# Batch 0 of a fused RWKV and low-rank-mixing kernel: V spread from two fp32r parts, and the last chunk's share of U·x added in 128-column pieces

## The chip, the cores and the metric

The kernel runs on one core of a Trainium2 chip. The metric is the device time of one execution in microseconds; lower is better. All engines named below are those of this core: PE (TensorE, with PEld for its weight loads), DVE (VectorE), ACT (ScalarE), POOL (GpSimd) and SP (SyncE), the last of which issues most DMAs.

## What is computed

There are 4 batches, 768 positions, 8 heads of 48 channels (so 384 channels), a hidden width of 1536 and a rank of 32. Cut to what matters, the reference is:

```
for t in range(S):                                   # attention, per batch and head
    y[t]  = r[t] @ (state + (u * k[t]) outer v[t])
    state = w * state + k[t] outer v[t]
x  = y as [batch, 768, 384]
h  = x^T @ U @ V                                     # U 768x32, V 32x768
u_ = x + h^T
out = u_ + relu(u_ @ w_ch1) @ w_ch2                  # 384 -> 1536 -> 384
```

U, V, w_ch1 and w_ch2 arrive as 64-bit floats and are turned into 32-bit ones on the chip; the outputs are 32-bit.

## The kernel before, in words

The positions of a batch are cut into 6 chunks of 128. For each chunk the attention is computed in products of chunk size: scores from r and k (`f_scores`, L1003), a masked copy of them (`am`, L1011), the change of the state (`f_state`, L1025), the product of masked scores with v (`f_out`, L1052) and of r with the carried state (L1058). DVE adds the two halves of a chunk's output to the term of u and writes x_0 to x_5 (L1071). Batch 0 has nothing to run beside it; the attention of batches 1 to 3 runs between products of the batch before.

What follows for a batch is low-rank mixing and then the two large products. G = U^T x (32 x 384) is summed over the chunks (`g_sum`, L1171): four products of 32 output rows each stand side by side in one PSUM bank, and in batch 0 the sum lies in the bank `wake`, which also takes filler products. `c_g` copies the four pieces into one SBUF tile `gf` and makes `Gs` of it, three blocks of 32 rows: G rounded to fp32r, the rest that rounding left, and the rounded G once more. `V3` (96 x 768) holds V in the same way in three blocks: rounded, rounded, rest. One product of K = 96 of `V3` and `Gs` then gives V·G almost as exactly as 32-bit inputs would. `c_x` transposes the chunks of x into banks (`pu`, and `bank_sc` and `bank_tr` for the second half of the batch), `c_xu` (`pu<-V,Gs`) adds V·G on top, ACT rounds the sum into `uTh` and DVE puts the rest into `uTl`. Those are the inputs of the first large product (`m_1`, `p1`), which takes three products per 128 x 128 block: weights high and low with `uTh`, weights high with `uTl`. ACT applies the relu (`hh`), DVE the rest (`hl`), and `m_2` (`p2`) multiplies by the second weights. The two halves of batch 0 (384 positions each) are t = 0 and t = 1.

V is loaded as a 128 x 192 tile (`raw_v`: 4 groups of 32 rows hold 192 columns of V each) and has to be spread to 32 x 768, three times over. `v_split` does that with four 32-bit products against `sel`, a 0-1 matrix, two for each half of V3; ACT casts a half and DVE subtracts the rounded block from the third.

Every weight tile that is loaded (`raw_w`) needs a byte pass (L605 on ACT or L601 on DVE), a scaling pass (L627, ACT) and two bit passes (L608 and L611, DVE) to become a 32-bit float, and then a cast (L645, ACT) and a subtraction (L646, DVE or POOL) to become a high and a low part, `w1s` or `w2s`.

The order of all engines is written out by a planner (`Plan.schedule`): the program records every operation with its key (`at(t, f)`), an estimated length and its buffers, and the planner lists the operations engine by engine as its estimates come out. It may choose POOL, DVE or ACT for operations that are given alternatives, and it puts filler products (`wake`, `wake2`) where it expects TensorE to idle. So a changed estimate or key moves operations far from the edit. Dependencies become semaphore waits; each engine runs its list strictly in that order.

## Time and profile before

| what | value |
|---|---|
| median of 3 runs | 400.66 us (399.52 to 400.8) |
| profiled execution, its own time | 400.29 us |
| its span, first to last instruction | 398.6 us |
| mean granted TensorE clock | 0.999 |
| PE busy | 389.6 us, 98% of the span |
| PEld busy | 374.7 us, 94% |
| DVE busy | 301.5 us, 76% |
| ACT busy | 143.8 us, 36% |
| POOL busy | 99.8 us, 25% |

The span is what the trace covers; the execution's own time is 1.7 us longer than it. A busy time is the sum of the stretches in which an engine executes at least one instruction; filler products count as busy, and successive products overlap, so that a product's listed length is longer than the distance to the next one. A share of the whole span says little of a single stage: in the first 50 us of this kernel, where batch 0's attention ends and its large products begin, the engines are used differently from the 350 us behind it.

### The profile page before, as it was taken

How to read it: one execution, taken by the hardware profiler on the slowest of the kernel's cores; microseconds unless marked ns; L12 is line 12 of the kernel's file. 1: busy time of each engine (PE TensorE's matmuls, PEld its weight loads, DVE VectorE, ACT ScalarE, POOL GpSimd, SP SyncE). 2: the span in 40 equal slices, each digit the busy share in tenths (PEclk: the TensorE clock that was granted, in tenths of full speed). 3: DMA queues.
4: the chain of work that ended last, by engine and by line, in shares of the span. 5: the costliest groups of instructions: out<-in, count | busy, mean ns of one | idle time of the engine just before them, and what ended most of it. 6: DMA issues, size and time to landing. Idle time of an engine off the chain costs nothing.

```text
span 398.6 us, 11762 instructions
## 1 busy us (share of the span) xinstructions
PE 389.6 (98%) x4815; PEld 374.7 (94%) x4815; DVE 301.5 (76%) x681; ACT 143.8 (36%) x372; POOL 99.8 (25%) x152
## 2 busy tenths in 40 slices
PE   7999999999999999999999999999999999999995
PEld 6897899999999999999999999999999999999994
DVE  5798999999999768888684588999444874555453
ACT  3557968467841312110133240241132422232220
POOL 2972142244422014131140131544000301100000
PEclk9999999999999999999999999999999999999999
DMA  9989998698769685785797777800126110000003
GB/s 143 177 174 276 176 222 191 107 231 213 133 99 198 99 193 78 124 134 81 147 168 111 150 167 114 136 6 3 61 46 137 57 62 0 2 0 2 0 0 127
DMA packets 189995, 45.28 MB, mean 114 GB/s; under 512 B 174702, under 2 KB 188399, under 8 KB 189935
## 3 DMA queue, kind: packets, MB, share of 16 engines
q1 hardware_dynamic: 186382, 43.28, 57.9%
q10 hardware_dynamic: 3552, 1.18, 1.4%
q8 instruction: 40, 0.66, 0.7%
q14 instruction: 21, 0.16, 0.2%
HBM read 36.77 MB, written 7.67 MB: 111 GB/s over the span
## 4 chain that ended last, share of the span: by engine, by line
PE 93%; DVE 3%; DMA 2%; SPq 0%; issue 0%; ACT 0%; DVEq 0%
PE p L385 63%; PE c L385 9%; PE pav L900 3%; PE pav L906 3%; PE bank_tr L385 2%; PE bank_sc L385 2%; DMA ld<-in_r_dram 2%; PE pav L1052 2%; PE bank_tr L1003 1%; PE bank_tr L880 1%; PE bank_tr L866 1%; PE bank_tr L1171 1%; PE pav L1058 1%; PE ptr L817 1%; DVE uTl L1235 1%; PE psu L1025 1%
## 5 line engine op out<-in xcount | busy, mean ns | idle before, releaser
L385 PE MATMUL p<-uTh,w1s 128*128 128x384 f32 x432 | 112.0, 339 | 0.2 <-DVE w1s L646 0.2
L385 PE MATMUL p<-w2s,hh 128*128 128x384 f32 x528 | 111.8, 339 | 0.2 <-ACT hh L1445 0.2
L385 PEld LDWEIGHTS p<-w2s,hh 128*128 128x128 f32 x528 | 92.3, 188 | 1.7 <-ACT hh L1445 0.7
L1445 ACT ACTIVATE hh<-p 128x384 fp32r<-128x384 f32 x72 | 35.4, 492 | 144.0 <-PE p L385 143.9
L385 PEld LDWEIGHTS p<-uTh,w1s 128*128 128x128 f32 x432 | 76.9, 188 | 1.3 <-DVE w1s L646 0.6
L385 PE MATMUL p<-uTl,w1s 128*128 128x384 f32 x216 | 72.5, 336 | 0.0
L1446 DVE SCALAR_TENSOR_TENSOR hl<-p,hh 128x384 fp32r<-128x384 f32 x72 | 39.9, 554 | 31.5 <-ACT hh L1445 30.7
L385 PE MATMUL p<-w2s,hl 128*128 128x384 f32 x264 | 62.3, 335 | 0.0
L385 PEld LDWEIGHTS p<-w2s,hl 128*128 128x128 f32 x264 | 47.3, 188 | 0.0
L385 PEld LDWEIGHTS p<-uTl,w1s 128*128 128x128 f32 x216 | 40.5, 188 | 0.3 <-DVE uTl L1235 0.3
L900 PEld LDWEIGHTS pav<-vsw,am 64*64 64x64 f32 x288 | 17.4, 134 | 4.5 <-issue 4.3
L1372 ACT ACTIVATE hh<-v 128x384 fp32r<-128x384 f32 x18 | 9.2, 526 | 34.4 <-DVE v L1363 31.7
L900 PE MATMUL pav<-vsw,am 64*64 64x48 f32 x288 | 19.8, 221 | 0.0
L1363 DVE TENSOR_TENSOR v<-c,s 128x384 f32<-128x384 f32 x18 | 9.9, 556 | 12.9 <-PE c L385 12.7
L900 PE MATMUL pav<-ldv,am 64*64 64x48 f32 x288 | 19.3, 221 | 0.0
L767 POOL MEMSET ks<- 128x128 f32 x24 | 4.8, 208 | 57.2 <-PE bank_tr L880 57.2
L906 PE MATMUL pav<-S,rT 48*64 48x48 f32 x528 | 19.1, 218 | 0.0
L1283 POOL TENSOR_TENSOR uTl<-ut,uTh 128x384 fp32r<-128x384 f32 x5 | 5.1, 1022 | 54.1 <-ACT uTh L1282 54.1
L385 PE MATMUL c<-uTh,w1s 128*128 128x384 f32 x72 | 18.5, 337 | 0.0
L777 POOL TENSOR_TENSOR dv<-ldr,ldk 128x384 f32<-128x384 f32 x13 | 13.3, 1022 | 20.4 <-DVE wm L528 8.8
L906 PEld LDWEIGHTS pav<-S,rT 48*64 48x64 f32 x528 | 17.3, 135 | 0.0
L900 PEld LDWEIGHTS pav<-ldv,am 64*64 64x64 f32 x288 | 17.0, 134 | 0.0
(240 smaller groups left out, 782.4 us busy)
## 6 DMA issues: line engine op xcount, KB each, us to landing
raw_w<-in_moe_w_ch_dram SPq DMA_DIRECT2D x24, 384.0 KB, 4.7
out_dram<-x SPq DMA_DIRECT2D x21, 192.0 KB, 2.9
ldr<-in_r_dram SPq DMA_DIRECT2D x20, 192.0 KB, 3.9
ldk<-in_k_dram SPq DMA_DIRECT2D x20, 192.0 KB, 4.8
ldv<-in_v_dram SPq DMA_DIRECT2D x20, 192.0 KB, 4.7
bl<-in_r_dram SPq DMA_DIRECT2D x79, 48.0 KB, 2.4
bl<-in_k_dram SPq DMA_DIRECT2D x79, 48.0 KB, 2.5
ub<-ud SPq DMA_DIRECT2D x15, 192.0 KB, 2.9
```

The lines of the kernel that those rows point to most:

```text
L385: return nc.tensor.matmul(*args, **kw)
L767: op("POOL", 250, lambda: nc.gpsimd.memset(ks.t[:, :, D:], 0.0), [(ks, "pad")], [])
L777: on_either(384, lambda e, a_=a_, b_=b_: e.tensor_mul(dv.t, a_()[:, :, :D], b_()[:, :, :D]), w_, r_, only="POOL" if front(n) else None)
L817: nc.tensor.transpose(pt.t[:PD, q * C:(q + 1) * C], src().rearrange("p h d -> p (h d)")[:, q * PE_:q * PE_ + PD], ident_)
L900: return nc.tensor.matmul(to(q, j, i), lhsT=am[j].t[half, q, :], rhs=vsw[n].t[half, q, :] if j else vt()[half, 2 * q, :], start=((alone or ...
L906: return nc.tensor.matmul(to(q, row, i), lhsT=rT.t[rows, q, i * C2:(i + 1) * C2], rhs=St[n, i].t[rows, q, :], start=False, stop=((alone or ...
L1052: return nc.tensor.matmul(avp[n][j].t[i * C2:(i + 1) * C2, q * D:(q + 1) * D], lhsT=ams[n][j].t[:, q, i * C2:(i + 1) * C2], rhs=vt()[:, 2 ...
L1283: on_either(384, lambda e: e.tensor_tensor(ul.t[:, ct, :], ut.t, f32(uh.t[:, ct, :]), ALU.subtract), [(ul, ct)], [ut, (uh, ct)])
L1363: on_dve(384, lambda e: e.tensor_tensor(to.t, pt.t[:, :TB], other.t, ALU.add), [to], [pt, other])
L1372: on_act(384, lambda: nc.scalar.activation(hh.t, value(), AF.Relu), [hh], [src])
L1445: on_act(384, lambda: nc.scalar.activation(hh.t, pt.t[:, :TB], AF.Relu), [hh], [pt])
L1446: on_dve(384, lambda e: e.scalar_tensor_tensor(hl.t, pt.t[:, :TB], 0.0, f32(hh.t), ALU.max, ALU.subtract), [hl], [pt, hh])
```

## The change

There are four parts.

1. **V.** `raw_v` is split into two fp32r parts, `v_parts` (ACT casts, POOL or DVE subtracts), and each half of V3 is the sum of four fp32r products of 192 columns, two for each part, against `sel` with blocks of zeros around the identity. What arrives in the bank is already (rounded, rounded, rest), so the cast by ACT is all that is left and DVE's subtraction falls away. The second half of V3 (t = 1) is recorded later, behind the first `p1`.
2. **G.** The sum over the chunks 0 to 4 is copied to `gf` before the last chunk is done (`c_g_sum`), and one 32-bit product against `sel` writes it three times into a bank (`pG_0` in `bank_tr`). When x_5 is there, three 32-bit products of 128 columns add the last chunk (`c_g_last`), and `Gs` is cast by ACT and finished by DVE column piece by column piece. `c_xu` of batch 0 waits for its own piece and its own half of V3.
3. **The first `p1`** takes its products in another order, those with the late low parts last.
4. **Estimates and keys.** The planner's lengths for several TensorE operations are raised (103 to 116 a transposition, 500 to 550, 520 to 600, 1000 to 1060), the keys of `G` and V are moved, the refill uses the still tile, and the chunks of batches 2 and 3 are recorded 3 us later.

```diff
-    Uf = cbuf([128, NCH, 1, R], F32, "Uf")
+    Uf = cbuf([128, NCH + 2, 1, R], F32, "Uf")
-    sel = wbuf([128, 3 * 128], F32, "xh", NXS, "sel")
+    sel = big([128, 128 // R, 6, R], F32R, "sel")
...
         def v_split(fl, raw):
-            for j in range(S // DM):
+            vp = big([128, 2, NV], F32R, "v_parts")
+            on_act(NV, lambda: nc.scalar.copy(vp.t[:, 0], fl()), [(vp, 0)], [raw])
+            on_either(NV, lambda e: e.tensor_tensor(vp.t[:, 1], fl(), f32(vp.t[:, 0]), ALU.subtract), [(vp, 1)], [raw, (vp, 0)])
+
+            def half(j):
                 pt = bank("acc", f"pv_{j}")
...
-                        whole(pt.t[:3 * R, i * NV:(i + 1) * NV],
-                              lhsT=sel.t[:, c * 3 * R:(c + 1) * 3 * R], rhs=fl(),
-                              start=(i == 0), stop=(i == DM // NV - 1), skip_group_check=True)
+                        for k, b0 in enumerate((3, 0)):
+                            whole(pt.t[:3 * R, i * NV:(i + 1) * NV], lhsT=sel.t[:, c, b0:b0 + 3], rhs=vp.t[:, k],
+                                  start=(i + k == 0), stop=(i + k == DM // NV), skip_group_check=True)
...
-                on_dve(384, lambda e, sl=sl, pt=pt: e.tensor_tensor(V3.t[2 * R:, sl], pt.t[2 * R:3 * R, :DM],
-                                                                    f32(V3.t[2 * R:, sl]), ALU.subtract), [(V3, j)], [pt])
+            half(0)
+            v_rest.append(lambda: half(1))
...
+    def c_g_sum():
+        w4 = DM // 4
+        gf = wbuf([R, DM], F32, "xl", NXS, "gf_0")
+        for g in range(4):
+            on_act(96, lambda g=g: nc.scalar.copy(gf.t[:, g * w4:(g + 1) * w4], wk.t[g * R:(g + 1) * R, 128:128 + w4]),
+                   [(gf, g)], [(wk, "g")])
+        pt = bank("tr", "pG_0")
+        pg.append(pt)
+        pe(700, lambda: whole(pt.t[:3 * R, :DM], lhsT=f32(sel.t[:R, 0, 2:5]), rhs=gf.t, start=True, stop=False, skip_group_check=True),
+           [(pt, ct) for ct in range(NCT)], [gf, sel])
+
+    def c_g_last():
+        n, pt = NCH - 1, pg[0]
+        three = Uf.t[:, n:].rearrange("p c o r -> p (c o r)")
+        G = Gs[0] = wbuf([3 * R, DM], F32R, "Gs", 1, "Gs_0")
+        for ct in range(NCT):
+            cs = slice(ct * 128, (ct + 1) * 128)
+            pe(235, lambda cs=cs, ct=ct: whole(pt.t[:3 * R, cs], lhsT=three, rhs=xs[n].t[:, cs], start=False, stop=(ct == NCT - 1),
+                                               skip_group_check=True), [(pt, ct)], [Uf, xs[n]])
+            on_act(128, lambda cs=cs: nc.scalar.copy(G.t[:, cs], pt.t[:3 * R, cs]), [(G, ct)], [(pt, ct)])
+            on_dve(128, lambda e, cs=cs: e.tensor_tensor(G.t[R:2 * R, cs], pt.t[R:2 * R, cs], f32(G.t[R:2 * R, cs]), ALU.subtract),
+                   [(G, ct)], [(pt, ct)])
...
+        if (b, t, f) == (0, 0, 0):
+            for ct, k in ((0, 0), (1, 0), (0, 2), (2, 0), (1, 2), (2, 2)):
+                pe((2 - k // 2) * MM, lambda ct=ct, k=k: part(ct, (2,) if k else (0, 1)), [pt], [((ul if k else uh), ct), W1[f]])
...
-    UV, GX, UVC = -84.9, (3, 33.0), (25.0, 33.0)
+    UV, GX, UVC = -84.9, (3, 32.0), (25.0, 31.6)
...
-                at(t, lambda n=n: a_chunk(n))
+                at(t + (0, 0, 3, 3)[b], lambda n=n: a_chunk(n))
...
+            at(end - 3, c_g_sum)
+            at(end, c_g_last)
+            at(t + 1.9, lambda: v_rest[0]())
```

What the planner makes of it is shown at three places. In the rows the number at a tile's end is its buffer's; 0 to 5 before it, in x, am, kT, ld and pav, is the chunk.

The first place is ACT while PE computes chunks 4 and 5 of batch 0. kT is the copy of a chunk's transposed k, without which the scores of that chunk can't start; L605 and L627 are the first two passes over a loaded tile. Before:

```order
L840 COPY kT_4_507<-ptk_4_489 112x512
L605 ACTIVATE raw_u_395<-raw_u_395 128x192
L627 ACTIVATE raw_u_395<-raw_u_395 128x192
L605 ACTIVATE raw_v_425<-raw_v_425 128x192
L627 ACTIVATE raw_v_425<-raw_v_425 128x192
L1041 ACTIVATE SW_4_567<-S_4_554,wmf_155 112x48 x4
L840 COPY kT_5_599<-ptk_5_583 112x512
L651 COPY Uf_617<-raw_u_395 128x192
L605 ACTIVATE raw_w1_0_477<-raw_w1_0_477 128x384
L627 ACTIVATE raw_w1_0_477<-raw_w1_0_477 128x384
```

Now:

```order
L605 ACTIVATE raw_u_378<-raw_u_378 128x192
L846 COPY kT_4_496<-ptk_4_479 112x512
L627 ACTIVATE raw_u_378<-raw_u_378 128x192
L605 ACTIVATE raw_v_398<-raw_v_398 128x192
L627 ACTIVATE raw_v_398<-raw_v_398 128x192
L1047 ACTIVATE SW_4_546<-S_4_544,wmf_158 112x48 x4
L605 ACTIVATE raw_w1_0_455<-raw_w1_0_455 128x384
L627 ACTIVATE raw_w1_0_455<-raw_w1_0_455 128x384
L846 COPY kT_5_593<-ptk_5_575 112x512
L652 COPY Uf_91<-raw_u_378 128x192
L653 COPY Uf_91<-raw_u_378 128x64
```

kT_5 stood ahead of the first weight tile's two passes and now stands behind them; kT_4 likewise stands behind one pass over raw_u.

The second place is PE from the end of chunk 5's attention to the first product of V3 and Gs; wake2 is a filler. Before, without the ten rows of transpositions into pu and bank_sc that stand between the two pieces:

```order
L385 MATMUL pv_0_742<-raw_v_425,sel_103 96x192 x2
L385 MATMUL pv_1_752<-raw_v_425,sel_103 96x192 x2
L1171 MATMUL wake_101<-x_5_748,Uf_617 32x96 x4
```

```order
L385 MATMUL pu0_0_2_787<-ident_69,x_2_473 128x128
L385 MATMUL wake2_794<-V3_756 128x512
L385 MATMUL bank_tr_88<-ident_69,x_4_663 128x128
L385 MATMUL bank_sc_89<-ident_69,x_5_748 128x128
L385 MATMUL pu0_1_1_774<-ident_69,x_5_748 128x128
L385 MATMUL bank_tr_88<-ident_69,x_5_748 128x128
L385 MATMUL wake2_794<-V3_756 128x512
L385 MATMUL pu0_0_0_766<-V3_756,Gs_0_791 128x384
```

Now, with the semaphores that each waits for:

```order
L385 MATMUL bank_tr_88<-gf_0_683,sel_104 96x384 [waits Activation_49]
L385 MATMUL bank_sc_89<-ident_69,x_3_561 128x128
L385 MATMUL bank_sc_89<-ident_69,x_4_657 128x128
L385 MATMUL bank_tr_88<-x_5_738,Uf_91 96x128 [waits DVE_49]
L385 MATMUL pv_0_753<-v_parts_728,sel_104 96x192 [waits Activation_49]
L385 MATMUL pv_0_753<-v_parts_728,sel_104 96x192 [waits Pool_49]
L385 MATMUL pv_0_753<-v_parts_728,sel_104 96x192 x2
L385 MATMUL bank_tr_88<-x_5_738,Uf_91 96x128 [waits Activation_49]
L385 MATMUL bank_tr_88<-x_5_738,Uf_91 96x128 [waits DVE_49]
```

The nine transpositions of t = 0, one filler of 128 columns and `pu<-V3,Gs` follow. The second and third column pieces of the last chunk's sum wait for ACT and DVE to be done with the first, and everything behind them on PE with them. The transpositions of t = 1 and its three products with V3 and Gs, which stood ahead of the first p1, now stand behind the second p1, and the second half of pv between the two.

The third place is ACT from its last passes over early weight tiles to the first uTh. Before:

```order
L627 ACTIVATE raw_w2_1_615<-raw_w2_1_615 128x384
L665 CAST V3_756<-pv_0_742 96x384
L665 CAST V3_756<-pv_1_752 96x384
L1191 COPY gf_0_771<-wake_101 32x96 x4
L1193 CAST Gs_0_791<-gf_0_771 32x384
L1196 CAST Gs_0_791<-gf_0_771 32x384
L645 CAST w1s_0_804<-raw_w1_0_477 128x384
L645 CAST w1s_1_806<-raw_w1_1_494 128x384
L1234 CAST uTh_0_0_813<-pu0_0_0_766 128x384
```

Now:

```order
L1206 COPY gf_0_683<-wake_102 32x96 x4
L605 ACTIVATE raw_w2_1_570<-raw_w2_1_570 128x384
L657 CAST v_parts_728<-raw_v_398 128x192
L627 ACTIVATE raw_w2_1_570<-raw_w2_1_570 128x384
L605 ACTIVATE raw_w1_2_605<-raw_w1_2_605 128x384
L627 ACTIVATE raw_w1_2_605<-raw_w1_2_605 128x384
L1222 CAST Gs_0_759<-bank_tr_88 96x128
L671 CAST V3_763<-pv_0_753 96x384
L1222 CAST Gs_0_759<-bank_tr_88 96x128 x2
L646 CAST w1s_0_780<-raw_w1_0_455 128x384
L646 CAST w1s_1_788<-raw_w1_1_471 128x384
L1263 CAST uTh_0_0_794<-pu0_0_0_767 128x384
```

The copies of gf moved ahead of the last chunk, and two tiles' passes and the cast of V's high part now stand between them and the first piece of Gs. On DVE (no rows) the two subtractions of V3 and one byte pass are gone from the same stretch, three short pieces of Gs stand where one of 384 columns stood, and the three uTl of t = 1 moved behind the third weight tile's passes.

## Rows read from the trace of the kernel before

**Rows 1.** Waits of PE: engine, tile, line, releaser: us in total, times, longest.

```profile
PE pu L385 <- DVE Gs L1194: 0.5, 1, 0.5
```

**Rows 2.** Busy time by stretch: stretch, length, busy (instructions) by engine, clock, DMA share, GB/s.

```profile
33.00:48.00 15.00, 13.62 (x132) 11.75 (x129) 13.70 (x31) 12.07 (x31) 1.62 (x5) 1.00 1.01 217
48.00:100.00 52.00, 52.00 (x698) 50.45 (x697) 51.08 (x119) 34.93 (x100) 18.87 (x25) 1.00 0.91 193
...
390.00:399.00 9.00, 3.63 (x21) 3.19 (x19) 2.14 (x4) 0.53 (x1) 0.00 (x0) 0.93 0.28 98
```

**Rows 3.** The chain of waits, 33 to 48 us: start, us, what.

```profile
35.64 0.62 DVE x L1071 x2
...
37.23 1.03 DVE V L666 x2
...
40.31 0.43 PE pu L385
...
40.76 0.49 ACT uTh L1234
...
46.96 0.48 DVE w1s L646
```

**Rows 4.** Timeline of PE, 15 to 33 us: start, us, instruction, tile shapes, count.

```profile
15.50 0.49 PE L385 MATMUL wake<-still 128*128 128x128 f32 x2
15.90 0.43 PE L817 MATMUL ptr<-ident,ld 128*112 128x128 f32 x2
...
30.48 0.37 PE L1003 MATMUL bank_tr<-rT,kT 48*128 48x128 f32 x1
```

**Rows 5.** Timeline of ACT, 29 to 38 us; in brackets idle time before, and its releaser.

```profile
29.11 0.57 ACT L840 COPY kT<-ptk 112x512 f32<-112x512 f32 x1
...
29.85 0.57 ACT L605 ACTIVATE raw_w<-raw_w 128x384 int32<-128x384 uint8 x1
30.32 0.55 ACT L627 ACTIVATE raw_w<-raw_w 128x384 f32<-128x384 f32 x1
30.79 0.57 ACT L605 ACTIVATE raw_w<-raw_w 128x384 int32<-128x384 uint8 x1
...
34.45 0.56 ACT L605 ACTIVATE raw_w<-raw_w 128x384 int32<-128x384 uint8 x1 [1.40 <-DMA raw_w<-in_moe_w_ch_dram]
...
37.45 0.95 ACT L1191 COPY gf<-wake 32x96 f32<-32x96 f32 x4
```

**Rows 6.** Timeline of PE, 33 to 48 us.

```profile
33.84 0.20 PE L1052 MATMUL pav<-ldv,am 128*64 128x48 f32 x1 [0.65 <-issue]
33.98 0.33 PE L385 MATMUL bank_tr<-ident,x 128*128 128x128 f32 x1
34.24 0.67 PE L1052 MATMUL pav<-ldv,am 128*64 128x48 f32 x16
...
35.45 1.59 PE L385 MATMUL pv<-raw_v,sel 128*96 128x192 f32 x8
36.97 0.37 PE L1171 MATMUL wake<-x,Uf 128*32 128x96 f32 x8
...
37.99 0.93 PE L385 MATMUL pu<-ident,x 128*128 128x128 f32 x7
38.67 0.48 PE L385 MATMUL wake<-V 96*128 96x512 f32 x1
...
41.44 0.51 PE L385 MATMUL p<-uTh,w1s 128*128 128x384 f32 x2
...
42.17 0.51 PE L385 MATMUL p<-uTh,w1s 128*128 128x384 f32 x2
42.52 0.33 PE L385 MATMUL p<-uTl,w1s 128*128 128x384 f32 x1
...
46.91 0.34 PE L385 MATMUL p<-uTh,w1s 128*128 128x384 f32 x1
47.48 0.44 PE L385 MATMUL p<-uTh,w1s 128*128 128x384 f32 x1 [0.24 <-DVE w1s L646]
```

More of the change, by code (lines that the diff above doesn't have):

```diff
@@ L634, in rwkv_moe @@
     BANKS = [None] * 26
+    v_rest, pg = [], []
     def weight_units():
@@ L820, in a_tr @@
         for q in range(0, NP, m):
-            pe(103 * m, lambda q=q: turn(q, q + m), [pt], sb)
+            pe(116 * m, lambda q=q: turn(q, q + m), [pt], sb)
         def by_pair():
@@ L1004, in product @@
                                     start=True, stop=True)
-        pe(1000, lambda: in_turn(*([lambda q=q, j=j: product(q, j) for q in range(NP)] for j in range(2))), abs_[n], [rT, kT],
+        pe(1060, lambda: in_turn(*([lambda q=q, j=j: product(q, j) for q in range(NP)] for j in range(2))), abs_[n], [rT, kT],
            tiled=True)
@@ L1172, in g_sum @@
                                  rhs=xs[n].t[:, g * w4:(g + 1) * w4],
-                                 start=(c0 == 0 and n % NCH == 0), stop=(n % NCH == NCH - 1), skip_group_check=True)
+                                 start=(c0 == 0 and n % NCH == 0), stop=(n % NCH == NCH - (1 if n >= NCH else 2)), skip_group_check=True)
     def c_gx(*ns):
@@ L1181, in c_g @@
         w4 = DM // 4
-        if b:
-            bank_ = bank("tr", f"pG_{b}")
-            pt, c0 = bank_, 0
-            pe(1000, lambda: g_sum(bank_, 0, range(b * NCH, (b + 1) * NCH)), [pt], [Uf] + [xs[b * NCH + c] for c in range(NCH)],
-               tiled=True)
-        else:
-            bank_, pt, c0 = wk, (wk, "g"), 128
+        bank_ = bank("tr", f"pG_{b}")
+        pt, c0 = bank_, 0
+        pe(1000, lambda: g_sum(bank_, 0, range(b * NCH, (b + 1) * NCH)), [pt], [Uf] + [xs[b * NCH + c] for c in range(NCH)],
+           tiled=True)
         gf = wbuf([R, DM], F32, "xl", NXS, f"gf_{b}")
@@ L1432, in m_1, with part @@
         pt = bank("mm", f"p1_{b}_{t}_{f}")
-        def part(ct):
+        def part(ct, terms):
             wt = W1[f].t
@@ L1437, in part @@
             o = pt.t[:, :TB]
-            whole(o, lhsT=wt[:, 0, fs], rhs=uh.t[:, ct, :], start=(ct == 0), stop=False)
-            whole(o, lhsT=wt[:, 1, fs], rhs=uh.t[:, ct, :], start=False, stop=False)
-            whole(o, lhsT=wt[:, 0, fs], rhs=ul.t[:, ct, :], start=False, stop=(ct == NCT - 1))
-        for ct in range(NCT):
-            pe(3 * MM, lambda ct=ct: part(ct), [pt], [(uh, ct), (ul, ct), W1[f]])
+            for k in terms:
+                whole(o, lhsT=wt[:, k == 1, fs], rhs=(ul if k == 2 else uh).t[:, ct, :], start=(ct + k == 0),
+                      stop=(ct + k == NCT + 1))
+        if (b, t, f) == (0, 0, 0):
+            for ct, k in ((0, 0), (1, 0), (0, 2), (2, 0), (1, 2), (2, 2)):
+                pe((2 - k // 2) * MM, lambda ct=ct, k=k: part(ct, (2,) if k else (0, 1)), [pt], [((ul if k else uh), ct), W1[f]])
+        else:
+            for ct in range(NCT):
+                pe(3 * MM, lambda ct=ct: part(ct, (0, 1, 2)), [pt], [(uh, ct), (ul, ct), W1[f]])
         hh = xbuf([128, TB], F32R, "hh", NH, f"hh_{b}_{t}_{f}")
@@ L1622, in rwkv_moe @@
     fill = waking(wk)
-    def refill():
-        whole(wk2.t, lhsT=V3.t[:, :128], rhs=V3.t[:, :512], start=True, stop=True, skip_group_check=True)
+    refill = waking(wk2)
     def at(t, f):
@@ L1634, in rwkv_moe @@
     UB = -88.5
[L1635 removed]
+    DVK, DV = 1, -1.0
     LATE_DG = 4
@@ L1648, in rwkv_moe @@
     at(-98, lambda: on_act(384, lambda: nc.scalar.copy(
-        sel.t.rearrange("p (c k r) -> p c k r", k=3, r=R),
-        ident_.rearrange("p (c r) -> p c r", r=R).unsqueeze(2).broadcast_to([128, 128 // R, 3, R])), [sel], []))
+        sel.t[:, :, 2:5], ident_.rearrange("p (c r) -> p c r", r=R).unsqueeze(2).broadcast_to([128, 128 // R, 3, R])),
+                           [(sel, 2)], []))
+    for i, n_ in ((0, 2), (5, 1)):
+        at(-50, lambda i=i, n_=n_: on_dve(128 * n_, lambda e: e.memset(f32(sel.t[:, :, i:i + n_]), 0.0), [(sel, i)], []))
     at(UB, load_ub)
@@ L1717, in rwkv_moe @@
             end = attention(b, t0, per, 5.0, 0)
-        at(end, lambda b=b: c_g(b))
+        if b:
+            at(end, lambda b=b: c_g(b))
         if b == 0:
-            at(end + 0.9, lambda: again.append(pe(220, refill, [wk2], [xs[NCH - 1], V3])))
+            at(end - 3, c_g_sum)
+            at(end, c_g_last)
+            at(t + 1.9, lambda: v_rest[0]())
+            at(end + 0.9, lambda: again.append(pe(214, refill, [wk2], [xs[NCH - 1]])))
             at(end + 1, lambda: c_xu(0, 0))
```

21 lines of the change are left out of this document (11 added, 10 removed).

## The prediction

> **What bounds the kernel now.** I read the waits of PE first: in the whole span behind the start-up it waits for another engine's data for long at one place only, 0.5 us for Gs [rows 1]. The busy times by stretch say where PE has time to give: from 48 us on it is busy without a gap (52.00 of 52.00), while 33 to 48 holds 13.62 of 15.00, fillers included [rows 2]. So only what happens ahead of 48 us can move the end, by as much as it lets PE reach one and the same instruction sooner. As that mark I take the second product of the third weight tile's p1, at 47.48 us [rows 6]: both programs have done the same work when they pass it. The chain of waits shows what leads there: x_5, then DVE's two subtractions of V3 (1.03), the first V·G product at 40.31, uTh at 40.76, and DVE again until w1s at 46.96 [rows 3]. PE's own timeline shows a filler at 38.67, 0.65 us of idle time without a named releaser ahead of 33.84, and fillers at 15.50 [rows 4, 6].
>
> **The change part by part.** I follow the engines to the mark; times are of the profiled execution (400.29 us, 0.37 below the median 400.66).
>
> *Front, down 0.4, then up 0.9.* The pair of fillers at 15.50 holds PE 0.40 us [rows 4] and is not in the new list there. That is lost again at chunk 5. kT_5 now stands behind both passes over the first weight tile. The first of these started at 29.85 and the second ended its turn at 30.79; a kT copy takes 0.57 [rows 5], so kT_5 is done at 31.36 and the scores start at 31.4 where they started at 30.48 [rows 4]: 0.9 later. Nothing says that the tile landed only at 29.85, since ACT came free just then; had it landed by 29.1, where kT_5 started before, kT_5 would start at 30.05 and the delay be 0.15. I take 0.9, because the later tile's pass at 34.45 did wait for its load [rows 5]: loads arrive barely in time here. A wait of kT_4 for raw_u's first pass is smaller and ends inside this one.
>
> *The unnamed stall, down 0.65.* PE stood 0.65 us at "issue" [rows 6], and the operations around that place have no semaphore to wait for. PE now comes 0.9 later, and the transposition that follows is gone from there. I take the stall as past by then; the other end is that it stays whole.
>
> *The transposition among chunk 5's products, down 0.26* (33.98 to 34.24 [rows 6]); it is repaid below. Chunk 5 then ends at 35.45 + 0.9 - 0.65 - 0.26 = 35.4, as before, and x_5 is done at 36.2 as before [rows 3]. The new U·x work costs x_5 nothing, since it stands behind it.
>
> *From 35.4 to the first p1.* The row of pv is the price of 32-bit products: 8 passes of 192 columns in 1.52 us, 0.19 each, two to a product [rows 6]. So the new gf product (384 columns) takes 0.76, each piece of U·x (128) 0.25. A transposition takes 0.1 (7 in 0.68 [rows 6]). No fp32r product of 192 columns is in the trace: at most it takes the 0.19 of such a pass, at least half of the 0.175 that a 384-column one takes (two in the 0.35 us from 42.17 to 42.52 [rows 6]); I take 0.1, near the lower end, which is the same format. PE then has: gf to 36.2, two transpositions to 36.4, piece 0 to 36.65, four V products to 37.05. ACT gets from the gf copies (0.95 [rows 5], about 33.6 to 34.55) through four passes of 0.47 and one short cast to 36.7, so it is barely free when piece 0 arrives: 0.45 from a product's start to ACT's start [rows 3], 36.85; done 37.1 at 0.25 a short cast. Pieces 1 and 2 follow at 37.15 and, behind DVE's first piece, 37.45; nine transpositions end at 38.6, a filler at 38.8, and the first V·G product starts at 38.8 instead of 40.31. ACT's and DVE's other pieces are ready by 38.9, before PE needs them. uTh starts 0.45 later, takes 0.49, and p1 starts at 39.8 instead of 41.44: **1.6 earlier**.
>
> *What now stands behind it: up 1.5.* The second half of V (0.4), six transpositions (0.6) and t = 1's three V·G products (0.52) were done ahead of 41.44 and are now between p1 and the mark. The cheaper V and the 32-bit products of G cancel inside these sums: 1.52 becomes 0.8, and 0.3 of U·x (36.97 to about 37.27) becomes 1.5.
>
> *Waits that go: down 0.6.* In the first p1 the products with uTl start late: 41.44 to 42.17 is 0.73 for three products of 0.175, 0.2 lost; the new order puts 0.35 of other work there. At the mark 46.91 to 47.48 is 0.57 for one product, 0.4 lost to w1s [rows 6]. DVE's list up to that w1s loses V3's 1.03, a byte pass and three uTl; so DVE, last at 46.96 before, is done over 1.5 us sooner and PE no longer waits.
>
> *Free of charge:* V's low part lies on POOL, idle from 33 to 41 (busy 1.62 of 15 [rows 2]); without that cover it would be 0.4 on DVE. The clearing of sel falls into DVE's wait for the first loads. The 3 us later chunks of batches 2 and 3 and the other moved rows lie in PE's gapless stretch: at nothing, or up to 0.5 if a wait opens.
>
> Sum: -1.6 + 1.5 - 0.6 = **-0.7 us: 399.6**, which is 1.1 (0.27%) under the median. 0.3% of the median, 1.2 us, is about what a measurement of this kernel can tell from no change.
>
> **The rivals.**
>
> *A: the unnamed stall stays, or finds another place.* For it: the operation had no semaphore to wait for, so what held it may be tied to its place in the program. Price 0.65 at 33 us, which x_5 and then all of the chain pass on: 400.29 - 0.7 + 0.65 = 400.2.
>
> *B: DVE's chain, not PE's work, sets the mark.* Then V3's 1.03, a byte pass and the three uTl (1.4) out of its 11.2 us from x_5 to w1s count in full: about -1.9, 398.4. Against it: PE's own work between 35.4 and the mark doesn't shrink. Part of it would come true if kT_5 costs only 0.15.
>
> *C: the pieces don't overlap.* All three pieces of U·x and the running casts share one bank. If piece, cast and subtraction follow each other singly, each round takes 0.25 + 0.28 + 0.25 + 0.25, about 1.0, so three end at 39.4 where my pipeline has 38.4, and the nine transpositions behind piece 2 start 1.15 later: 400.29 - 0.7 + 1.15 = 400.7, slower than before. It decides if piece 2 waits for anything behind the first piece's subtraction. The Trainium skill, "PSUM — Partial Sum Buffer", section "PSUM bank collisions raise a hardware error", says that engines must be kept apart by bank and group of 32 partitions and not by address, which speaks against pieces in one bank. The new rows agree with it halfway (piece 1 waits for ACT, piece 2 for DVE); no run here shows a collision.
>
> *D: the clock falls.* The long fillers on V3 are gone and PE has short gaps from 36 to 40. The granted clock is 1.00 throughout 33 to 48 and 0.93 only where PE runs out of work at the end (3.63 busy of 9.00 [rows 2]). At 1.2 instead of 2.4 GHz the 2.7 us of work between 36.4 and 39.8 would take twice as long: 400.29 - 0.7 + 2.7 = 402.3, slower. It needs PE much emptier than my 0.8 us of gaps. The Trainium skill, "TensorE: Matmul & The Clock Gate", Part 1, has the half clock as the state that activity lifts; by that rule a thinner stretch could cost these 2.7 us.
>
> **How the numbers follow.** Forecast 0.58 (399.0 to 400.1 by its own terms: kT_5's other end, V products at 0.19, a late wait), A 0.18, B 0.12, C 0.07, D 0.05. Under 399.45 lie B and about half of the forecast: faster 0.40. Over 401.85 lie D and, if the stall stays and new waits open later too, a part of A and C: slower 0.10. The rest, 0.50, is within 0.3%. The range from 398.4 to 401.2 takes in the forecast, A, C and the edge of B.
>
> **What would show it.** kT_5's copy on ACT starting near 30.8 and the scores near 31.4; no stall of 0.6 us in chunk 5's products; V products 0.1 us apart; the first V·G product near 38.8 and p1 near 39.8; no wait for w1s after it. Wrong if the first V·G product starts after 39.5, if PE waits behind p1, or if the clock is under 1.00 before 48 us.

## The result and the profile after

The changed kernel is slower: median 405.73 us of 5 runs (402.54 to 406.17) against 400.66 (399.52 to 400.98), a ratio of 1.0112 [1.0075, 1.0149]. The prediction was 399.6 (398.4 to 401.2). The profiled execution is the fastest of the five: 402.54 us, span 400.7, mean granted clock 0.998; the other four show mean clocks of 0.992 to 0.996.

The page's busy times of the kernel after (busy us, share of the span, instructions):

```profile
PE 392.1 (98%) x4813; PEld 376.4 (94%) x4813; DVE 301.6 (75%) x679; ACT 142.4 (36%) x365; POOL 104.1 (26%) x153
```

Nothing there explains 5 us. The busy times by stretch do (columns as in [rows 2]):

```profile
33.00:48.00 15.00, 14.27 (x163) 12.31 (x152) 13.84 (x32) 13.49 (x35) 3.62 (x10) 1.00 0.99 226
48.00:100.00 52.00, 50.56 (x687) 48.50 (x686) 48.98 (x113) 29.30 (x78) 24.07 (x29) 1.00 0.80 168
```

In the stretch that the prediction worked through, 33 to 48 us, PE is fuller than before, 14.27 us against 13.62. In 48 to 100, which was gapless before (52.00), it now idles for 1.44 us. The waits of PE name two new ones, both bigger than anything between chunk 5 and the end was before [rows 1]:

```profile
PE p L385 <- issue: 0.8, 1, 0.8
PE p L385 <- DVE x L1116: 0.7, 1, 0.7
PE bank_tr L385 <- DVE Gs L1223: 0.4, 1, 0.4
PE bank_tr L385 <- ACT Gs L1222: 0.2, 1, 0.2
```

Its timeline, 85 to 93 us, places them (start, us, instruction; in brackets the idle time before and its releaser):

```profile
87.45 0.59 PE L385 MATMUL p<-uTh,w1s 128*128 128x384 f32 x2 [0.69 <-DVE x L1116]
...
91.12 0.44 PE L385 MATMUL p<-uTh,w1s 128*128 128x384 f32 x1
92.32 0.45 PE L385 MATMUL p<-uTh,w1s 128*128 128x384 f32 x1 [0.76 <-issue]
```

In the list of PE's instructions this is the part where the attention of batch 1 runs between batch 0's large products. The blocks of chunk 8 and chunk 9 (counted through the batches) are 128 short products each. Before, 36 large products stand between the two blocks: a p1, a p2, a p1 and a p2 of 9 products each. Now the two p2 stand behind chunk 9, and only 18 products are left between. The diff shows no such move; it comes out of the planner. The chain of waits tells what the first of the two waits hangs on (start, us, what):

```profile
84.97 0.06 PE bank_tr L886
85.06 0.36 DVE S L1149
85.41 0.66 DVE am L1121 x2
86.08 0.53 DVE x L1116 x2
86.61 0.32 DVE S L1149
86.94 0.37 DVE x L1116
87.31 0.14 issue
87.45 1.83 PE p L385 x9
```

DVE needs 2.2 us behind chunk 8's block to finish S, am and x; PE has nine large products (84.91 to 86.76) in that time, and the next one needs what x releases. The second wait has no releaser, "issue".

The new front, where the prediction was at work, in PE's timeline:

```profile
33.38 1.15 PE L1058 MATMUL pav<-ldv,am 128*64 128x48 f32 x32
...
35.07 0.88 PE L385 MATMUL bank_tr<-gf,sel 32*96 32x384 f32 x2
...
36.16 0.38 PE L385 MATMUL bank_tr<-x,Uf 128*96 128x128 f32 x2
36.30 0.59 PE L385 MATMUL pv<-v_parts,sel 128*96 128x192 f32 x4
37.14 0.46 PE L385 MATMUL bank_tr<-x,Uf 128*96 128x128 f32 x2 [0.25 <-ACT Gs L1222]
37.98 0.46 PE L385 MATMUL bank_tr<-x,Uf 128*96 128x128 f32 x2 [0.38 <-DVE Gs L1223]
...
39.40 0.77 PE L385 MATMUL pu<-V,Gs 96*128 96x384 f32 x3
...
40.38 0.99 PE L385 MATMUL p<-uTh,w1s 128*128 128x384 f32 x4
...
42.33 0.52 PE L385 MATMUL pv<-v_parts,sel 128*96 128x192 f32 x4
...
47.57 0.51 PE L385 MATMUL p<-uTh,w1s 128*128 128x384 f32 x2
```

The mark, the second product of the last row, is at 47.74 (47.57 plus one product of 0.17), against 47.48. Chunk 0's first scores stood at 9.97 in this execution and at 8.52 before; e1 below, of the same kernel, has them at 8.41, and e13 at 9.98, so a late start is an accident of an execution and not of the change. It shrinks on the way: chunk 5's scores start at 31.32 here and at 30.79 in e5, which starts at 8.40 and has the same lists up to there. Here is the account of the profiled executions, 402.54 - 400.29 = 2.25 us: the mark 0.26 later; from the mark to PE's last product 347.65 instead of 345.82, so 1.83 more; behind it 0.16. Of the 1.83, 1.45 are the two waits.

### The profile page after: what moved, and what is told of

Read it like the earlier page. It is cut to its first block, busy times and chain, and to the rows that moved or that the text cites. A ratio compares the mean times of both kernels' runs of the same rounds, so it can differ in the third digit from the quotient of the medians.

```text
span 400.7 us, 11756 instructions
## 1 busy us (share of the span) xinstructions
PE 392.1 (98%) x4813; PEld 376.4 (94%) x4813; DVE 301.6 (75%) x679; ACT 142.4 (36%) x365; POOL 104.1 (26%) x153
## 4 chain that ended last, share of the span: by engine, by line
PE 88%; SPq 6%; ACT 1%; DMA 1%; DVE 1%; issue 1%
PE p L385 64%; PE c L385 9%; SPq L723 4%; PE pav L906 3%; PE pav L912 3%; PE bank_tr L385 2%; PE bank_sc L385 2%; PE bank_tr L886 1%; DMA raw_w<-in_moe_w_ch_dram 1%; SPq L580 1%; PE bank_tr L872 1%; PE bank_tr L1177 1%; PE bank_sc L872 1%; PE bank_tr L823 1%; PE pu L385 1%
## 5 line engine op out<-in xcount | busy, mean ns | idle before, releaser
L1479 DVE SCALAR_TENSOR_TENSOR hl<-p,hh 128x384 fp32r<-128x384 f32 x72 | 39.9, 554 | 31.4 <-ACT hh L1478 30.5
L783 POOL TENSOR_TENSOR dv<-ldr,ldk 128x384 f32<-128x384 f32 x17 | 17.3, 1020 | 11.9 <-DVE kT L812 4.2
L1162 ACT ACTIVATE SW<-S,wm 112x48 f32<-112x48 f32 x56 | 14.1, 323 | 16.5 <-DVE S L1149 16.5
L1519 DVE TENSOR_TENSOR x<-p,x 128x384 f32<-128x384 f32 x28 | 14.1, 549 | 4.6 <-PE p L385 4.5
```

Of the source, the lines that this page charges most:

```text
L783: on_either(384, lambda e, a_=a_, b_=b_: e.tensor_mul(dv.t, a_()[:, :, :D], b_()[:, :, :D]), w_, r_, only="POOL" if front(n) else None)
L1162: nc.scalar.activation(dec.t[:, q], new.t[:, q], AF.Copy, scale=wm.t[:, q])
L1479: on_dve(384, lambda e: e.scalar_tensor_tensor(hl.t, pt.t[:, :TB], 0.0, f32(hh.t), ALU.max, ALU.subtract), [hl], [pt, hh])
L1519: on_dve(384, lambda e, x=x, pt=pt: e.tensor_tensor(x.t, pt.t[:, :DM], x.t, ALU.add), [x], [pt])
```

## The experiments

Three places were open: the front up to 48 us, the waits at 87 to 93 us, and whatever the other executions had that this one hadn't. The first theory (P in the expectations) was that the loss sits in the order, in the moved rows behind 48 us; the rivals were the clock (K), and later the work on V and G ahead of 48 us (F).

**e1_again: the changed kernel, unaltered.**

> The changed kernel once more, unaltered, because its profiled execution (402.54) was the fastest of its five and the other four (404.99 to 406.17) showed a lower mean granted clock (0.992 to 0.996 for 0.998). Theory P (the planner's order: two PE gaps of 0.69 and 0.76 us between 86 and 93 us) expects the same two gaps in this profile, and a span that differs from 400.7 by under 1 us. Theory K (the clock) expects a span of 402.5 to 404.5 and, beside the two gaps, stretches in which fillers and products take twice their time or in which the granted clock is under 1.00; which stretch that is decides where to look.

405.06 us (403.74 to 406.91), ratio 1.0139 [1.0108, 1.017]. The granted clock is 1.00 in every stretch from 12 to 390 us, so K finds nothing in this execution; its span of 401.9 is 1.2 above the first, a little more than P allowed. Its waits show that the two numbers of the first profile are not fixed, and that a third wait belongs to the kernel:

```profile
PE p L385 <- issue: 1.7, 1, 1.7
...
PE bank_tr L1009 <- ACT kT L846: 0.9, 1, 0.9
...
PE p L385 <- DVE x L1116: 0.7, 1, 0.7
```

The wait for x is the same 0.69, the one at "issue" 1.73 instead of 0.76. The wait for kT is chunk 4's, and the chain of waits of the same run has its reason:

```profile
21.63 4.65 DMA raw_u<-in_moe_U_dram
...
26.30 0.02 ACT raw_u L605
...
26.57 0.58 ACT kT L846
...
27.20 0.37 PE bank_tr L1009
```

kT_4 stands behind raw_u's first pass on ACT, and that waited 3.93 us for U's load, to 26.30. Before, kT_4 ran at 24.25 while the load was still on its way. With its early start and this wait, e1 reaches the mark at 47.71; the first profile had the late start, which hid the wait, and reached it at 47.74.

**e2_before_est and e11_before_est2: the kernel before with the new lengths and the 3 us** (two runs of one program).

```diff
-            pe(103 * m, lambda q=q: turn(q, q + m), [pt], sb)
+            pe(116 * m, lambda q=q: turn(q, q + m), [pt], sb)
...
-                at(t, lambda n=n: a_chunk(n))
+                at(t + (0, 0, 3, 3)[b], lambda n=n: a_chunk(n))
```

and likewise 1000 to 1060, 500 to 550, 520 to 600.

> The kernel before with the raised lengths alone (116, 1060, 550, 600) and the chunks of batches 2 and 3 recorded 3 us later; V, G and p1 as before. Theory P expects a part of the loss here already: new PE gaps between 48 and 390 us, 1 to 2 us slower than the kernel before (401.5 to 402.5). Theory K expects no loss from lengths as such: within 1 us of the kernel before, clock 0.999.

> The kernel before with the raised lengths and the 3 us (as e2_before_est), to stand beside e9_both_fixed on one chip: what is left between the two is V, G and p1. By the prediction's own terms for those (1.6 earlier at p1, 1.5 of moved work, 0.6 of waits gone) e9_both_fixed would be 0.4 to 0.7 below this one; if they are worth nothing, the two agree within 0.5 at 399.3 to 400.

399.56 us, ratio 0.9997 [0.9976, 1.0019], and 399.79, 0.9991 [0.9972, 1.001]. The estimates alone do nothing that the median shows, and 48 to 390 us stays without a gap. But they do two things that the medians hide. They put kT_4 behind raw_u's first pass, here without any of the change's code; in e11, where that pass starts at 26.93, PE waits for it, in e2 (25.39) it doesn't:

```profile
PE bank_tr L1003 <- ACT kT L840: 1.1, 1, 1.1
```

So e2 reaches the mark at 47.06 and e11 at 48.07. And from the mark to the last product they take 345.12 and 345.08, 0.7 less than before's 345.82. e2 and e11, not the kernel before, are the measure for what V, G and the first p1 are worth.

**e3_after_oldest: the change with the old lengths and without the 3 us**, the same lines the other way round.

> The changed kernel with the old lengths (103, 1000, 500, 520) and without the 3 us; V, G, p1 and the keys as changed. Theory P expects the gaps of 0.69 and 0.76 between 86 and 93 us to go and the time to fall by about 1.5 below the changed kernel's median. Theory K expects the runs at 404 to 406 with a clock under 0.997 to stay, since the work on TensorE before 45 us is the same.

404.25 us, ratio 1.0092 [1.0058, 1.0125]. P expected the two gaps to go and 1.5 less. The time is 1.5 under the first measurement, 0.8 under e1, but the gaps did not go: 18 large products stand between the blocks here too. kT_4 is ahead of raw_u's pass again, and the mark is at 47.07, 0.4 ahead of before. All of that and more is lost behind it, at the 0.68 for x, a wait of 2.25 us at "issue" (92.72) and a half clock behind it. So the loss comes with the three code parts and their keys, not with the estimates. **e4_before_again** is the kernel before, run once on the same chip.

> The kernel before once more, for a second profile of its first 12 us: its products went to full speed at about 5.3 us, the changed kernel's at about 10.2, with the same TensorE instructions up to there. If the start is chance, this profile may show either; if the change moved it, this one shows 5.3 again and chunk 0's scores at 8.5.

399.77 us, chunk 0's scores at 8.69, mark at 47.56, and behind it only the gap of 0.23 at 173 us that the first profile of before has too.

**e5_vparts_own_ring: one buffer taken from another ring.** The planner hands out the tiles of a ring in recorded order. The change puts v_parts into `big`, the ring of the weight tiles, so weight tiles wait for others to come free, and a p2 is not ready when the planner comes to the place between the blocks.

```diff
-            vp = big([128, 2, NV], F32R, "v_parts")
+            vp = wbuf([128, 2, NV], F32R, "xh", NXS, "v_parts")
```

> The changed kernel with v_parts in the small ring that sel has left (xh) and not among the weight tiles. Up to 41 us ACT's and PE's lists are those of the changed kernel; behind it, 36 large products stand between the blocks of chunk 8 and chunk 9 as in the kernel before, where the changed kernel has 18. Theory S (spacing: two blocks of short products too close to each other, so that PE waits for instructions at 91 us and for DVE's x at 87) expects no gap over 0.2 us between 48 and 100 us, PE busy 52 of 52 there, a clock of 0.998 or more in nearly all runs, and 399.5 to 401. Theory F (the loss lies in the V and G work ahead of 48 us) expects what the changed kernel has, 404 to 406, since that work is untouched.

400.09 us (398.44 to 401.38, 10 runs), ratio 1.0000 [0.9986, 1.0014]. The lists are the change's up to 41 us, and 36 large products stand between the blocks again. The busy times by stretch:

```profile
48.00:100.00 52.00, 52.00 (x699) 50.49 (x698) 50.34 (x118) 33.96 (x96) 19.01 (x24) 1.00 0.92 195
```

One allocation brings back 5.0 us (405.06 to 400.09). The gap is closed, and V's and G's new way is still in place.

**e6, e7, e8: the number between the blocks, set by a weight tile's load.** If that number is what counts, it must give the loss with v_parts where the change has it, and in the kernel before as well. In each the time at which one to three loads are recorded is shifted. e6, on the change, has 27 between the blocks:

```diff
-T0 + use[i] * PER - 6 - LEAD, load)
+T0 + use[i] * PER - 6 - LEAD + (0.8 if i in (18, 20) else 0), load)
```

e7 is e3 with the same for loads 18, 19 and 20, and has 36. e8 is the kernel before, one load earlier, and has 27:

```diff
+T0 + use[i] * PER - 6 - LEAD + (-2 if i in (18,) else 0), load)
```

> The changed kernel with v_parts where it was and the loads of the first weight tiles number 8 and 9 recorded 0.8 us later, behind the splitting of the second weight tile number 6 in the ring of weight tiles. That alone puts 27 large products between the blocks of chunk 8 and chunk 9 (18 changed, 36 before); nothing ahead of 80 us moves. Theory S expects a part of the loss to go: no wait for DVE's x, a gap at issue under 0.7 us or none, 400 to 402.5. Theory F expects 404 to 406.

> The changed kernel with the old lengths (as in e3_after_oldest) and the loads of weight tiles 8 and 9 recorded 0.8 us later: 36 products between the two blocks, and kT_5 ahead of the weight passes. Theory S expects all of e3_after_oldest's loss to go and its front (the mark at 47.07 where the kernel before has 47.48) to be kept: no gaps from 48 to 100 us, 398.8 to 400.2, a little under the kernel before. Theory F expects 403 to 405 as in e3_after_oldest.

> The kernel before with one key moved: the load of the first weight tile number 8 is recorded 2 us earlier, so that 27 and not 36 products stand between the blocks of chunk 8 and chunk 9; V, G and all work ahead of 60 us as before. Theory S expects about what e6_after_27 shows in that stretch, a gap at issue between 0 and 0.7 us at 90 to 93 us and 400 to 402. Theory F expects the time of the kernel before, 399.9 to 400.7.

e7, with 36: 400.95 us, ratio 1.0012 [0.9999, 1.0025], no gap from 48 to 100 us. e3's loss is gone. e8, the kernel before with 27, is 401.03 us, 1.0012 [0.9994, 1.0029]; the time does not tell it from before, but its timeline has a stall that neither profile of before shows:

```profile
92.57 0.20 PE L880 MATMUL bank_sc<-ldv,ks 64*48 64x48 f32 x1 [0.92 <-issue]
```

e6, the change with 27, is 403.82 us, 1.0079 [1.0063, 1.0096], a miss: the wait for x is gone, but the time hardly fell. Its profiled execution, the slowest of its runs, has 1.90 us at "issue" (95.79), 1.35 for kT_4 (27.96), and 0.41 and 0.66 for parts of weight tiles (123.17, 124.27), which its moved loads may have made. 27 is thus not enough, and the kT_4 wait needs a test of its own.

**e10_kt4_only: the change with kT_4 ahead of raw_u's passes on ACT**, by a later estimate for U's load; no other list differs.

```diff
-late=LATER if big_one and len(landing) <= FIRST else LATE)
+late=(LATER if big_one and len(landing) <= FIRST else LATE) + (800 if name == 'u' else 0 if name == 'w1_0' else 0))
```

> The changed kernel with U's load alone taken as 0.8 us later by the planner: kT_4 ahead of raw_u's pass on ACT, kT_5 still behind the passes over the first weight tile, and 18 products between the blocks of chunk 8 and chunk 9. Theory S with the second place expects the changed kernel's time less about 1 us, 403 to 404.5, with the gaps at 87 and 91 us unchanged (0.69 and 0.7 to 2.3) and no wait for kT_4. If kT_4 alone were the cause, 400 to 401.

403.38 us, ratio 1.0077 [1.0046, 1.0107]: 1.7 less than e1 (four runs each), though the interval overlaps that of the first measurement. kT_4 runs at 24.37. But the same wait turns up one chunk on, behind the first weight tile's load, and the mark is at 47.93, no sooner than e1's 47.71; so the profile doesn't show where the 1.7 come from:

```profile
31.72 0.37 PE L1009 MATMUL bank_tr<-rT,kT 48*128 48x128 f32 x1 [0.98 <-ACT kT L846]
```

**e9_both_fixed: e5 with both copies moved**, U's load 0.8 and the first weight tile's 0.6 later in the planner's estimate (the line above with 600 for w1_0).

> e5_vparts_own_ring, and the planner is told that U's load lands 0.8 us later and that of the first weight tile 0.6 us later, so that on ACT kT_4 stands ahead of the first pass over raw_u and kT_5 ahead of the passes over the first weight tile, as in the kernel before; 36 products between the blocks of chunk 8 and chunk 9. Theory S with the second place (PE waited 0.88 us for kT_4 in e1_again and 1.35 in e6_after_27, because ACT stood at raw_u's load) expects no wait of PE for kT in any run, the mark at 46.5 to 47.1 whatever the start does, no gap from 48 to 100, and a median of 398.5 to 399.6, 0.5 to 1.4 under e5_vparts_own_ring. If kT_4 were of no weight, it is e5_vparts_own_ring's 400.1.

402.28 us, ratio 1.0051 [1.0032, 1.007]: a miss. Some of PE's large products moved with it, from 73 us on, and new waits for weight parts opened (0.30 for w2s at 116.26, 0.65 for w1s at 119.05). It tests something else than it was made for, and its time says nothing of kT.

**e12_quiet: the change, every list as it is, with the loads held back.** What is the wait at "issue"? A core's program arrives in packets too: the changed kernel's page has them among its queues (packets, MB, share of 16 engines):

```profile
q8 instruction: 40, 0.66, 0.7%
```

That is some 16 KB each. In e1 one of them starts at 90.90 us and takes 0.97, and PE stands from 91.50 to 93.23:

```profile
q8 instruction: 1, 0.02, 30.2%
```

(the DMA view of 90.8 to 91.0 us; the share is of 16 engines in 0.2 us.) The theory (Q in the expectation): the packet comes late because it lies among the loads, 314 GB/s in 90 to 92 us; the rival: PE would stand there anyway. The edit makes one weight tile's load, and with it five loads behind it, wait for the first large product behind chunk 9.

```diff
+                    if name == "w1_8":
+                        tc.add_manual_dep(mine[0].ins, behind9[0].ins.name,
+                                          mybir.DependencyInfo(mybir.DependencyClass.Sync, mybir.DependencyReason.DATA),
+                                          reason="not beside the block of chunk 9")
```

> The changed kernel with its list of instructions unaltered on every engine; the load of the first weight tile number 8 is made to wait for the first large product behind the block of chunk 9, so that SP issues it and the five loads behind it at about 91.3 us and not from 87.6. Theory Q (PE's instructions come late because their packet stands in the DMA queues among these loads) expects 88 to 91 us with DMA far under the 350 GB/s of e1_again, the gap at issue under 0.3 us instead of 0.76 to 1.73, the wait for DVE's x unchanged at 0.69, and a median 1 to 2.5 us under the changed kernel's 405, unless tiles 8 and 9 then come late. Theory D (the packet comes late whatever else the queues carry, since two dense blocks follow each other) expects the gap at issue as before, 0.7 to 2.3, and 404 to 406.

Of the busy times by stretch, first e1's and then e12's (the last column is GB/s):

```profile
90.00:92.00 2.00, 1.50 (x86) 1.19 (x77) 2.00 (x7) 1.38 (x5) 2.00 (x2) 1.00 1.00 314
92.00:94.00 2.00, 0.77 (x4) 0.77 (x5) 1.88 (x7) 1.24 (x6) 2.00 (x5) 1.00 1.15 196
```

```profile
90.00:92.00 2.00, 2.00 (x38) 1.75 (x40) 2.00 (x5) 0.87 (x4) 0.00 (x0) 1.00 0.03 8
92.00:94.00 2.00, 2.00 (x116) 1.95 (x108) 2.00 (x7) 1.40 (x5) 1.73 (x2) 1.00 0.00 0
...
30.00:31.00 1.00, 1.00 (x9) 0.66 (x9) 1.00 (x3) 0.19 (x1) 0.66 (x1) 0.50 0.93 349
```

With 8 GB/s beside it the packet lands unnoticed, and PE runs on through the same instructions without a gap. It starts at 91.17, 0.38 ahead of the block of chunk 9, and takes 0.96; in e1 it starts 1.75 behind the block's first product and takes hardly longer, so it is the start that came late there. In the first profile the packet starts in time, at 89.03, but takes 1.89. The wait for x stays, 0.69 (89.79). So the two waits have different causes: x is late by the order, the packet with the traffic (one profile of e12 against three of the same list with a gap: after, e1 and e10).

That PE stands for the packet shows in all traces: in each of the nine waits at "issue" of 0.41 to 2.25 us behind the start-up (before, after, e1, e3, e6, e7, e8 twice, e10) PE goes on 1.32 to 1.46 us after the last such packet has landed. And all nine are at one of two places: counted over PE's products, weight loads and semaphore instructions in the trace, behind number 1217 (at 33 us) or behind 2753 or 2754 (at 92 us), in seven kernels alike. The places are 1536 or 1537 apart, six times 256; 40 packets for some 9,700 such instructions are about 240 each, an estimate from the page's counts. The unnamed stall of [rows 6] is one of the nine: its packet is under way from 31.50 to 32.52, and PE goes on at 33.84.

Traffic alone does not do it: before has 250 GB/s at 88 to 90 us, where its packet starts (89.52), and no gap. It has 36 large products between the blocks, as e5 has, and so large products among the 256 instructions ahead of the place: these take 4.94 us in before (from 87.85) and 4.46 in e5. In e1 they are the block of short products and little else, 2.35 us to where PE stands (89.15 to 91.50). So the order halves the time that a packet has; beside those loads that was too short, without them (e12) it was enough. The halving is counted from the traces, not tested by itself. The time of e12 is 403.89 us, 1.0077 [1.0053, 1.0101], only 1.2 under e1's: kT_4's wait is still there, and there are new waits (0.35 at 128.88, 0.16 at 123.59), probably because the loads were held back. In its profiled execution, its slowest, kT_4's wait is 1.30 us, and the granted clock falls to 0.50 behind it.

The Trainium skill, "Runtime: NRT & Kernel Launch", section "Instruction fetch mechanics", has the program fetched in blocks of 16 KiB and calls the cost of crossing one "mostly hidden". The size agrees with q8's packets. From 48 us on they are hidden in before, e5 and e12; not in the changed kernel (0.76 and 1.73), e3 (2.25), e6 (1.90), e8 (0.92) and e10 (1.54).

**e13_36_kt4: e5 and e10's exchange together**, nothing else moved (e10's line on e5).

> e5_vparts_own_ring with one exchange on ACT, kT_4 ahead of the first pass over raw_u, and every list else the same; kT_5 still behind the passes over the first weight tile. If a wait for kT_4 costs e5_vparts_own_ring's other runs what it cost e1_again and e6_after_27 (0.9 to 1.35), the median falls from 400.1 to 399.0 to 399.8 and no PE wait for kT_4 is in the profile. If the wait only moves to kT_5, which ACT can't start before the weight tile has landed, it stays within 0.4 of 400.1 and the profile shows PE waiting for kT about 0.9 ahead of chunk 5's scores, as in e10_kt4_only (0.98 at 31.72).

399.68 us (398.84 to 400.42, 10 runs), ratio 0.9984 [0.997, 0.9997], beside 400.14 for before. Its busy times, 27 us on:

```profile
27.00:33.00 6.00, 6.00 (x163) 5.42 (x159) 6.00 (x15) 4.56 (x14) 3.40 (x5) 1.00 0.85 273
...
48.00:100.00 52.00, 52.00 (x698) 50.48 (x698) 50.34 (x119) 33.86 (x95) 18.96 (x24) 1.00 0.89 194
```

No wait for kT, no gap from 48 us on, although this execution started late (9.98). It is 0.46 us or 0.16% under before, barely more than its interval. Against e5's ratio of 1.0000 the intervals overlap, so that the exchange itself is worth 0.4 us is likely, not shown. They also overlap with those of e2 (0.9997) and e11 (0.9991), which have the new lengths and none of the code parts: no run shows that V, G and the first p1 gain anything.

## Why the prediction was wrong

*The step that failed.* "The 3 us later chunks of batches 2 and 3 and the other moved rows lie in PE's gapless stretch: at nothing, or up to 0.5 if a wait opens." The 3 us cost nothing (e2). The other moved rows cost nearly all of the loss: e1 less e5 is 5.0 us in the median, made by one buffer's ring. (Of the two profiles of the changed kernel, each the fastest of its runs, the first takes 2.5 more than e5 from the mark to the last product, the other 3.4.) The prediction took a stretch that was gapless under the old order for one that stays gapless under a new one. The order of the rows was there to be read beforehand: half of the products between two blocks of short ones was gone, and with them what DVE's 2.2 us and the instruction packet had been hidden behind.

*The second step that failed.* "A wait of kT_4 for raw_u's first pass is smaller and ends inside this one." It is 0.88 in e1, 1.35 in e6, 1.30 in e12. It was not smaller, since kT_4 stood 1.4 us ahead of the pass before (24.25 and 25.66) and the pass starts when its load has landed. It did not end inside the other one either: kT_5 runs at 30.92 in e1 and at 30.17 in e5, which has the same ACT list without the wait. The place comes with the new lengths (e2 and e11 have it, e3 has not), which the prediction did not price. In e6 and e12 the half clock behind it makes it dearer: in e12 from the scores of chunk 4 to those of chunk 5 it is 5.80 us (28.05 to 33.85) where e13 takes 4.24 (27.21 to 31.45). What it costs in the median is open: e10 is 1.7 under e1, e13 only 0.4 under e5, and these are no further parts of the 5.0.

*The third step that failed: the sum for the front.* The -0.7 stands for the way from the end of chunk 5's products to the mark, since the prediction has chunk 5 end as before. Before, that way is 12.03 us (35.45 to 47.48, and the same in e4 and e8). With the change it is 12.67 in the first profile (35.07 to 47.74) and 12.42 in e1, e5 and e13: 0.4 to 0.6 more and not 0.7 less. PE's timeline of e5, from chunk 5's end to the row of the mark:

```profile
34.56 0.88 PE L385 MATMUL bank_tr<-gf,sel 32*96 32x384 f32 x2
...
39.62 1.00 PE L385 MATMUL p<-uTh,w1s 128*128 128x384 f32 x4
...
46.81 0.51 PE L385 MATMUL p<-uTh,w1s 128*128 128x384 f32 x2
```

p1 comes 5.06 us behind chunk 5's end there, for 5.99 before: 0.9 sooner instead of 1.6. From p1 to the mark it takes 1.3 more instead of 0.9. The following paragraphs say which terms.

*The front, step by step.* On ACT's timeline kT_5's copy started at 30.70 (predicted 30.8) behind the weight tile's passes, and chunk 5's scores at 31.32 (31.4):

```profile
30.25 0.54 ACT L627 ACTIVATE raw_w<-raw_w 128x384 f32<-128x384 f32 x1
30.70 0.57 ACT L846 COPY kT<-ptk 112x512 f32<-112x512 f32 x1
```

The place behind the passes is as predicted; the times are so by luck, since this execution started 1.45 late. In e5, which didn't, they are 30.17 and 30.79, near the other end that the prediction named (30.05): the delay of chunk 5 is 0.3, not 0.9.

The unnamed stall of [rows 6] is gone, as predicted: 32 products run as one row at 33.38, with no transposition inside. But V, G and p1 are not what took it away: e4, the kernel before, has only 0.13 of it, and e7, with them and the old lengths, has 0.42. V's four products take 0.59 with the last one's tail, so about 0.1 each; PE never waits for w1s at the mark.

*Mis-sized: the column pieces.* The prediction started them 0.3 apart. They are at 36.16, 37.14 and 37.98, so 0.98 and 0.84 apart: ACT casts a piece, then PE runs the next product, then DVE subtracts, then PE. DVE's timeline of the kernel after has the hand-over:

```profile
37.64 0.28 DVE L1223 TENSOR_TENSOR Gs<-bank_tr,Gs 32x128 fp32r<-32x128 f32 x1 [0.61 <-PE bank_tr L385]
```

DVE stood idle while the product of the next piece wrote the same bank, although its own piece was cast by 37.09. This is rival C's round (about 1.0 foreseen), at half its price: the third piece starts 0.53 behind the forecast, and 0.86 behind it if both are counted from chunk 5's end, which came 0.33 sooner than assumed. The first V·G product is at 39.40 (38.8 forecast; 40.31 before) and p1 at 40.38 (39.8; 41.44): 1.06 earlier instead of 1.6, of which 0.38 is the earlier end of chunk 5. In e5 they are at 38.64 and 39.62; there the second piece does not wait for ACT, and the pieces are 0.73 and 0.84 apart.

*Mis-sized: the waits that go.* From p1 to the mark it takes 7.36 where before took 6.04: 1.32 more, 0.9 forecast. The wait for w1s did go. The one for uTl did not: nine products from 40.38 to 42.33 are 1.95 us for 1.57 at 0.174 each, 0.38 lost where before lost 0.2, so the new order of the first p1 saved nothing here.

*What is left of the forecast.* e5's mark is at 46.98 and e3's at 47.07, 0.5 and 0.4 ahead of before, and e13, with both disturbances away, is 0.46 faster than before in the median. That looks like the -0.7, but by luck: two errors cancel. Chunk 5 is held up by 0.3 and not 0.9 and ends 0.89 sooner in e5, and what follows takes 0.4 more. And e2, with V, G and p1 as before, has its mark at 47.06:

```profile
46.88 0.51 PE L385 MATMUL p<-uTh,w1s 128*128 128x384 f32 x2
```

e13's mark, after a late start, is at 47.66, behind before's; its gain lies behind the mark (345.13 for 345.82), where e2 has the same (345.12).

*The rivals.* A did not come true at 33 us, yet it named the right thing: an "issue" wait is what came later, at a second place with a fixed count of instructions, so tied to a place in the program as A says. B did not: PE's row, not DVE's, sets the mark. C came true by half. D named the right danger at the wrong place: the clock is 1.00 from 33 to 48 us, and falls elsewhere, behind single waits; a PE much emptier than 0.8 us of gaps, which D asked for, it did not take: in e12 it fell behind one wait of 1.30.

*Open.* Counted from start to start, the two waits of the first profile cost 1.89 and not 1.45: 86.42 to 87.45 and 91.12 to 92.32, where a product in a row takes 0.17. That covers the 1.83 against before. Against e5 0.6 stays (2.49 less 1.89; in e1 3.42 less 2.85), which no wait over 0.15 shows. The changed kernel's other executions have no trace. Three mean clocks of the first measurement (0.992, 0.993, 0.993) fit a fall as in e3 (0.992), but that is argued, not shown; the fourth, 0.996, is also e1's, whose profile has no fall.

## What to carry to other kernels

Where a planner writes the order, a buffer's ring is part of the order: put a new short-lived tile into a ring that nobody waits for, and compare the lists of the whole program, not those around the edit. A stretch without gaps is gapless by the order it has; ask of each moved block what it used to stand behind, DVE's chain and the arrival of instructions included. A copy that releases PE should not stand behind a pass that waits for a load. And where a change brings new estimates with it, run the old code with them: without e2 the gain of the estimates would have passed for one of V and G.

## What was unexpected of the hardware

- **Instructions can come late.** A block of 128 short products uses them up in 1.9 us; where 18 or 27 long products stood ahead of it, and loads ran beside it, PE stood 0.76 to 2.25 us with nothing to wait for but "issue", and went on 1.3 to 1.5 us after a 16 KB instruction packet had landed. With 8 GB/s of loads it was 0 at the same instructions (e12).
- **The clock falls after some of such waits, not after all.** e3's busy times behind its 2.25 us (clock ahead of the last two columns):

```profile
92.00:93.00 1.00, 0.28 (x2) 0.19 (x2) 0.00 (x0) 0.00 (x0) 0.00 (x0) 0.69 1.10 146
93.00:94.00 1.00, 1.00 (x4) 1.00 (x4) 0.93 (x3) 0.66 (x2) 0.63 (x2) 0.50 0.37 66
94.00:95.00 1.00, 1.00 (x4) 1.00 (x4) 0.97 (x5) 0.36 (x1) 0.32 (x2) 0.50 0.97 196
```

  Granted is 0.50, the 1.2 GHz level, with PE fully busy and four products in a microsecond; it is 1.00 again by 96 us. The same stands behind waits of 1.90 (e6) and of 1.30 and 1.35 for kT_4 (e12, e6), but not behind e1's 1.73 or e10's 1.54. So one wait costs its own length in one execution and some 1.5 us more in another (e12 beside e13, above), which may be part of why the changed kernel's runs lie 402.54 to 406.91 and those of e13 398.84 to 400.42.
